# Softmax of a decode attention by chunk instead of by group: a lag of three steps between K and V, and cache reads in runs of 16 KB

## The chip, the cores and the metric

The kernel runs on one core of one Trainium2 chip. The metric is the device time of one execution, in microseconds (us). A time is the median of several runs; a ratio is the mean time of one kernel's fast runs over that of the other's fast runs of the same rounds, so it is not quite the ratio of the medians. The span of a profile is the profiled execution itself; the timed value of that execution is about 1.8 us longer in the two profiles compared.

## The reference, cut to what matters

One token is decoded through a transformer block: modulation, layer norm, attention over a long cache, and a gated feed-forward layer. The cache is nearly all of the data.

```python
B, Sq, D = (1, 1, 1024)
Hq, Hkv, Sk, Dh = (32, 4, 65536, 128)        # 8 query heads share one K/V head
...
sa, ca, ga, sb, cb, gb = ...                  # (silu(c) @ w_mod), six vectors
h = layernorm(x) * (1 + ca) + sa
q = (h @ wq)                                  # heads
scores = einsum('bhqd,bhkd->bhqk', q, k) * Dh ** (-0.5)
p = softmax(scores)
o = einsum('bhqk,bhkd->bhqd', p, v) @ wo
x = x + ga * o
h = layernorm(x) * (1 + cb) + sb
x = x + gb * ((gelu(h @ w_gate) * (h @ w_up)) @ w_down)     # F = 3584
```

K and V together are 134.2 MB in bf16; all inputs read are 185.6 MB.

## The kernel before

The cache of each of the four K/V heads (a "group") is cut into 8 chunks of 8192 keys: 32 K chunks and 32 V chunks of 2 MB. A step handles one K chunk and, `LAG` steps later, the V chunk of the same number. In each of the 16 units of a step, PE transposes four blocks of 128 keys (plus one extra "warm" matmul that is overwritten), DVE or ACT copies the result from PSUM to `kt`, PE multiplies it with the queries, and PE multiplies four V blocks with the probabilities.

```python
E_KEYS = 16                           # keys in a row on one partition: 16 * 128 * 2 B = 4 KB
CH = min(E_KEYS * P * 4, SK)          # 8192
LAG = NCH + 2                         # 10: exp needs the maximum of the whole group of 8 chunks
...
def kv_src(tensor_ap, i):
    g, cch = divmod(i, NCH)
    return tensor_ap[0, g, cch * CH:(cch + 1) * CH, :].rearrange(
        "(a p e) d -> p a (e d)", p=P, e=E_KEYS)
```

One queue issues every load in program order. Each load waits until its buffer is free, and what is behind it waits too:

```python
pro_rot = ["kb0", "kb1", "kb2", "wb0", "wb1", "vb0", "vb1", "vb2"]    # w_mod, wq, the first K chunks
kpool = ["kb0", "kb1", "kb2", "wb0", "wb1"]                           # later K chunks
for st, (ki, vi) in enumerate(steps):
    if ki is not None: ...addjob(("k", ki), ...)
    if vi is not None: addjob(("v", vi), f"vb{vi % 3}")               # V: three buffers
...
def issue(key, dst_fn, src_ap):
    wtv(sy, b.fsem, b.issued)         # the buffer's last user is done
    inst = sy.dma_start(dst_fn(b.t), src_ap)
```

The score copy is on ACT, and the exps of a group come in one burst, 8 of them over 512 columns:

```python
def scatter_copy(i):                  # ACT, once per K chunk
    inst = ac.activation(out=out_ap, in_=in_ap, func=ACT.Copy)
def emit_exp(g, h):                   # ACT, 8 per group
    inst = ac.activation(out=PT[g % 2][:, h, :], in_=S[g % 2][:, h, :], func=ACT.Exp,
                         bias=negm[...], scale=SCALE, accum_out=sums[...])
```

## Time and profile before

| | before |
|---|---|
| time, median of all 16 runs | 484.77 us |
| span of the profile | 482.5 us |
| mean rate of the loads over the span | 387 GB/s |
| steps of K alone | 10 |
| first V chunk used at | 142.1 us |

The first lines are from the page of the kernel before: the span in 40 slices of 12.06 us. A digit is the busy share in tenths, `DMA` is the mean of the 16 engines, `GB/s` is what they moved.

```profile
span 482.5 us, 18072 instructions
...
PE   1345299999779889879898888898898543164342
...
PEclk9999999999989999998799999889999555555555
DMA  8999999999974999999999999999998999999994
GB/s 312 421 423 418 412 408 407 407 408 407 406 289 157 409 408 399 407 408 407 408 407 407 404 400 407 408 408 406 407 376 330 383 410 409 402 418 418 410 387 161
```

The stream of loads is near its top nearly everywhere. The exceptions are slices 12 and 13 (289 and 157 GB/s, at 132.7 to 156.8 us), and weakly slices 30 to 32 (376, 330, 383). The same page has the kinds of work that matter here: line, engine, operation, tiles, shapes, count, busy time, mean ns, then the idle time before it.

```profile
L752 DVE CAST kt<-tb 128x512 bf16<-128x512 f32 x256 | 176.2, 691 | 115.3 <-PE tb L481 113.7
L926 ACT ACTIVATE kt<-tb 128x512 bf16<-128x512 f32 x256 | 150.6, 599 | 128.1 <-PE tb L481 128.0
L351 PE MATMUL pv<-PT,vb 128*128 128x8 bf16 x1536 | 101.5, 176 | 34.5 <-DMA vb<-in_A_v_cache_dram 30.1
...
L936 ACT ACTIVATE S<-sc 128x512 f32<-128x512 f32 x32 | 33.8, 1057 | 10.4 <-PE tb L351 9.6
...
L947 ACT ACTIVATE PT<-S,negm 128x512 bf16<-128x512 f32 x32 | 22.7, 711 | 1.6 <-DVE negm L776 1.6
```

The windows view gives the busy time of each engine in a stretch, with the number of instructions, the granted clock, the DMA share and the rate. These two are the stretch in which the stream starves, for the kernel before:

```profile
132.66:144.72 12.06, 9.56 (x176) 8.75 (x174) 6.39 (x10) 8.78 (x18) 0.00 (x0) 0.86 0.73 290
144.72:156.78 12.06, 12.06 (x298) 11.78 (x295) 8.86 (x16) 7.67 (x14) 0.00 (x0) 1.00 0.44 156
```

In the second one PE (the first busy time) is full for the whole window, while the DMA share is 0.44: here compute is what the stream waits for. The waits view of the load queue of the kernel before says on what (total us, times, longest):

```profile
SPq L299 <- PE pv L536: 184.1, 25, 22.2
```

The queue waited longest for the matmul that ends a V chunk, because the next V load wants that chunk's buffer.

### The profile page before, as it was taken

What the parts mean: (1) busy time and instruction counts of PE and PEld (TensorE: products, weight loads), DVE (VectorE), ACT (ScalarE), POOL (GpSimd) and SP (SyncE); (2) the same over time, 40 slices, a digit from 0 to 9 for tenths busy, and PEclk for the clock granted to TensorE, in tenths of its full rate; (3) what the DMA queues carried; (4) which work ended last, traced back from release to release, by engine and by line L of the source; (5) the groups of instructions that cost most, each with busy time, mean ns of one, the idle gap of its engine ahead of it and who ended that gap; (6) DMA issues with size and microseconds to landing.
All of it is one profiled execution on the core that took longest, in us unless ns stands there. A gap on an engine that the chain in (4) does not pass through costs nothing.

```text
span 482.5 us, 18072 instructions
## 1 busy us (share of the span) xinstructions
PE 345.8 (72%) x8243; PEld 326.6 (68%) x8243; DVE 212.3 (44%) x400; ACT 207.2 (43%) x361; POOL 2.3 (0%) x11
## 2 busy tenths in 40 slices
PE   1345299999779889879898888898898543164342
PEld 1344299998779788879798888798887543163332
DVE  0002068888657656556366565556655100020010
ACT  2000067776976555585355558555555500010000
POOL 0000000000000000000000000000000000000000
PEclk9999999999989999998799999889999555555555
DMA  8999999999974999999999999999998999999994
GB/s 312 421 423 418 412 408 407 407 408 407 406 289 157 409 408 399 407 408 407 408 407 407 404 400 407 408 408 406 407 376 330 383 410 409 402 418 418 410 387 161
DMA packets 46205, 186.77 MB, mean 387 GB/s; under 512 B 1584, under 2 KB 1584, under 8 KB 44080
## 3 DMA queue, kind: packets, MB, share of 16 engines
q1 hardware_dynamic: 46128, 185.61, 96.8%
q8 instruction: 65, 1.06, 0.9%
q14 instruction: 12, 0.10, 0.1%
HBM read 185.60 MB, written 0.00 MB: 385 GB/s over the span
## 4 chain that ended last, share of the span: by engine, by line
PE 54%; DMA 23%; issue 8%; SPq 8%; ACT 6%; DVE 1%; ACTq 0%; DVEq 0%
PE tb L351 30%; DMA vb<-in_A_v_cache_dram 9%; SPq L299 7%; PE sc L351 7%; DMA vb<-in_w_mod_dram 6%; PE pv L351 6%; PE tb L481 6%; DMA kb<-in_B_w_down_dram 4%; DMA kb<-in_A_k_cache_dram 4%; ACT PT L947 3%; ACT kt L926 3%; PE sc L504 2%; PE pv L536 2%; PE pr L351 1%; DVE kt L752 0%
## 5 line engine op out<-in xcount | busy, mean ns | idle before, releaser
L752 DVE CAST kt<-tb 128x512 bf16<-128x512 f32 x256 | 176.2, 691 | 115.3 <-PE tb L481 113.7
L926 ACT ACTIVATE kt<-tb 128x512 bf16<-128x512 f32 x256 | 150.6, 599 | 128.1 <-PE tb L481 128.0
L351 PE MATMUL pv<-PT,vb 128*128 128x8 bf16 x1536 | 101.5, 176 | 34.5 <-DMA vb<-in_A_v_cache_dram 30.1
L351 PE MATMUL sc<-qT,kt 128*128 128x8 bf16 x1536 | 112.4, 167 | 17.6 <-ACT kt L926 12.2
L351 PEld LDWEIGHTS pv<-PT,vb 128*128 128x128 bf16 x1536 | 83.3, 100 | 36.0 <-DMA vb<-in_A_v_cache_dram 31.1
L351 PE MATMUL tb<-ident,kb 128*128 128x128 bf16 x864 | 99.1, 225 | 3.7 <-issue 3.7
L351 PEld LDWEIGHTS sc<-qT,kt 128*128 128x128 bf16 x1536 | 80.9, 97 | 22.0 <-ACT kt L926 13.8
L504 PE MATMUL sc<-qT,kt 128*128 128x8 bf16 x512 | 85.1, 166 | 2.5 <-issue 2.5
L351 PE MATMUL tb<-kb,ident 128*128 128x256 bf16 x288 | 80.0, 278 | 4.1 <-DMA kb<-in_A_k_cache_dram 4.1
L536 PE MATMUL pv<-PT,vb 128*128 128x8 bf16 x512 | 79.7, 175 | 0.0
L351 PEld LDWEIGHTS tb<-ident,kb 128*128 128x128 bf16 x864 | 73.5, 99 | 8.5 <-issue 3.8
L481 PE MATMUL tb<-ident,kb 128*128 128x128 bf16 x288 | 65.0, 226 | 1.8 <-issue 1.8
L351 PE MATMUL tb<-ident,wb 128*128 128x128 bf16 x528 | 59.5, 222 | 1.9 <-issue 1.9
L536 PEld LDWEIGHTS pv<-PT,vb 128*128 128x128 bf16 x512 | 50.2, 98 | 2.1 <-issue 1.9
L504 PEld LDWEIGHTS sc<-qT,kt 128*128 128x128 bf16 x512 | 49.1, 96 | 2.0 <-issue 2.0
L351 PE MATMUL tb<-wb,ident 128*128 128x256 bf16 x176 | 48.2, 274 | 0.0
L351 PEld LDWEIGHTS tb<-ident,wb 128*128 128x128 bf16 x528 | 44.3, 98 | 4.2 <-issue 1.6
L481 PE MATMUL tb<-ident,wb 128*128 128x128 bf16 x176 | 39.3, 223 | 0.9 <-issue 0.9
L936 ACT ACTIVATE S<-sc 128x512 f32<-128x512 f32 x32 | 33.8, 1057 | 10.4 <-PE tb L351 9.6
L351 PEld LDWEIGHTS tb<-kb,ident 128*128 128x128 bf16 x288 | 28.0, 97 | 5.2 <-DMA kb<-in_A_k_cache_dram 4.2
L481 PEld LDWEIGHTS tb<-ident,kb 128*128 128x128 bf16 x288 | 29.1, 101 | 2.3 <-issue 2.3
L947 ACT ACTIVATE PT<-S,negm 128x512 bf16<-128x512 f32 x32 | 22.7, 711 | 1.6 <-DVE negm L776 1.6
(164 smaller groups left out, 258.4 us busy)
## 6 DMA issues: line engine op xcount, KB each, us to landing
vb<-in_A_v_cache_dram SPq DMA_DIRECT2D x32, 2048.0 KB, 14.1
kb<-in_A_k_cache_dram SPq DMA_DIRECT2D x18, 2048.0 KB, 22.5
wb<-in_A_k_cache_dram SPq DMA_DIRECT2D x11, 2048.0 KB, 20.2
wob<-in_A_wo_dram SPq DMA_DIRECT2D x4, 2048.0 KB, 18.4
vb<-in_A_k_cache_dram SPq DMA_DIRECT2D x3, 2048.0 KB, 25.5
kb<-in_B_w_gate_dram SPq DMA_DIRECT2D x3, 1792.0 KB, 21.0
vb<-in_B_w_up_dram SPq DMA_DIRECT2D x3, 1792.0 KB, 29.1
kb<-in_B_w_down_dram SPq DMA_DIRECT2D x3, 1792.0 KB, 20.9
```

Of the source, the lines that this page charges most:

```text
L299: inst = sy.dma_start(dst_fn(b.t), src_ap)
L351: inst = pe.matmul(*args, **kwargs)
L481: last = f(TB[tb][:, bb * P:(bb + 1) * P], tt[:, slot:slot + P], ident[:, :], start=True, stop=True)
L504: last = f(SC[scb][:, b * HPG:(b + 1) * HPG], kt[:, slot0 + bb * P:slot0 + (bb + 1) * P], qT[:, g * HPG:(g + 1) * HPG], start=True, stop=True)
L536: last = f(PVB[0][:, 0:HPG], tt[:, slot:slot + DH], PT[gv % 2][:, :, bq], start=first, stop=final)
L752: inst = dv.tensor_copy(kt[:, slot0:slot0 + BU * P], TB[tb][:, 0:BU * P])
L926: inst = ac.activation(out=kt[:, slot0:slot0 + BU * P], in_=TB[tb][:, 0:BU * P], func=ACT.Copy)
L936: inst = ac.activation(out=out_ap, in_=in_ap, func=ACT.Copy)
L947: inst = ac.activation(out=PT[g % 2][:, h, :], in_=S[g % 2][:, h, :], func=ACT.Exp, bias=negm[:, g * HPG + h:g * HPG + h + 1], scale=SCALE ...
```

## The change

Every chunk gets its own softmax: its own maximum, exps and partial V product, and the eight parts of a group are combined at its end with weights exp(m_c - M). V can then follow K after 3 steps instead of 10. The score copy goes from ACT to DVE. Each partition reads 64 keys in a row (16 KB) instead of four runs of 16 keys (4 KB). Loads of `w_gate` are put between the last V chunks.

```diff
-E_KEYS = 16
+E_KEYS = 64
-    CH = min(E_KEYS * P * 4, SK)
+    CH = min(E_KEYS * P, SK)
-    LAG = NCH + 2
+    LAG = 3
-    NKT = 8
+    NKT = 6
+    NSR = 2
+    NPR = 4
...
             if vi is not None:
+                if ki is None:
+                    addjob(("gate", gates_early), kpool[(kidx + 1 + gates_early) % len(kpool)])
+                    gates_early += 1
                 addjob(("v", vi), f"vb{vi % 3}")
...
-            for g in range(G):
+            for i in range(NKC):
                 inst = gp.partition_all_reduce(gmax..., rmax..., P, bass.bass_isa.ReduceOp.max)
...
-                    last = f(PVB[0][:, 0:HPG], tt[:, slot:slot + DH], PT[gv % 2][:, :, bq],
+                    last = f(GB[gv % 2][:, cv * HPG:(cv + 1) * HPG], tt[:, slot:slot + DH],
+                             PTR[vi % NPR][:, :, b], start=first, stop=final)
...
+            def chunk_sc_copy(i):                                   # DVE
+                inst = dv.tensor_copy(out_ap, in_ap)
...
+            def group_post(gv):                                     # DVE, about ten small operations
+                ... negM = min over chunks, wdel = negm - negM, wexp on ACT,
+                ... ow = sum(part * wexp), tw = sum(total * wexp), oT = ow / tw
...
-                inst = ac.activation(out=PT[g % 2][:, h, :], in_=S[g % 2][:, h, :], func=ACT.Exp,
+                inst = ac.activation(out=PTR[i % NPR][:, h, :], in_=SR[i % NSR][:, h, :], func=ACT.Exp,
```

More of the change, by code (lines that the diff above doesn't have):

```diff
@@ L85, in bass_adaLN_cond__gqa_block_cached__geglu_ffn__decode_kernel @@
     NKC = G * NCH
-    LAG = NCH + 2
+    LAG = 3
     NSTEPS = NKC + LAG
-    NKT = 8
+    NKT = 6
     NTB = 4
     SLAG = 3
+    NSR = 2
+    NPR = 4
     SCALE = float(DH) ** -0.5
     EPS = 1e-5
-    NBQ = SK // P
     WO_ROWS = HPG * DH
@@ L97, in bass_adaLN_cond__gqa_block_cached__geglu_ffn__decode_kernel @@
     assert CH <= STAGE_COLS
+    assert NCH * HPG <= 512
+    SC_COPY_AT = SLAG
+    CMAX_AT = SLAG + 1
+    NEGM_AT = SLAG + 3
+    EXP_AT = SLAG + 5
     with ExitStack() as es:
@@ L104, in bass_adaLN_cond__gqa_block_cached__geglu_ffn__decode_kernel @@
         sem_names = [
-            "misc", "gp", "gpmx", "pe", "dve", "act", "t2act", "t2dve", "ea", "ed", "sdone", "scdone",
+            "misc", "gp", "gpmx", "dve", "act", "t2act", "t2dve", "ea", "ed", "sdone", "scdone",
             "exp", "pr", "pv", "out",
@@ L124, in bass_adaLN_cond__gqa_block_cached__geglu_ffn__decode_kernel @@
         kt = sb("kt", [P, NKT * BU * P])
-        S = [sb(f"S{j}", [P, HPG, NBQ], FP32) for j in range(2)]
-        PT = [sb(f"PT{j}", [P, HPG, NBQ]) for j in range(2)]
+        SR = [sb(f"SR{j}", [P, HPG, NB], FP32) for j in range(NSR)]
+        PTR = [sb(f"PTR{j}", [P, HPG, NB]) for j in range(NPR)]
         x8 = sb("x8", [NI, P])
@@ L142, in bass_adaLN_cond__gqa_block_cached__geglu_ffn__decode_kernel @@
         stat = sb("stat", [P, 8], FP32)
-        rmax = sb("rmax", [P, G * HPG], FP32)
-        cmax = sb("cmax", [P, G * HPG], FP32)
-        gmax = sb("gmax", [P, G * HPG], FP32)
-        negm = sb("negm", [P, G * HPG], FP32)
-        sums = sb("sums", [P, G * HPG], FP32)
+        rmax = sb("rmax", [P, NKC * HPG], FP32)
+        gmax = sb("gmax", [P, NKC * HPG], FP32)
+        negm = sb("negm", [P, NKC * HPG], FP32)
+        sums = sb("sums", [P, NKC * HPG], FP32)
+        negM = sb("negM", [P, HPG], FP32)
+        wdel = sb("wdel", [P, NCH * HPG], FP32)
+        wexp = sb("wexp", [P, NCH * HPG], FP32)
+        cmb1 = sb("cmb1", [P, NCH * HPG], FP32)
+        cmb2 = sb("cmb2", [P, NCH * HPG], FP32)
+        ow = sb("ow", [P, HPG], FP32)
+        tw = sb("tw", [P, HPG], FP32)
         rtot8 = sb("rtot8", [P, HPG], FP32)
@@ L165, in bass_adaLN_cond__gqa_block_cached__geglu_ffn__decode_kernel @@
         SC = [pst(f"sc{j}") for j in range(2)]
-        PVB = [pst("pv")]
-        PR = [pst("pr")]
+        GB = [pst("gb0"), pst("gb1")]
         plan = {}
@@ L229, in bass_adaLN_cond__gqa_block_cached__geglu_ffn__decode_kernel @@
         kidx = None
+        gates_early = 0
         WO_AT_CV = max(0, NCH - 2)
@@ L249, in bass_adaLN_cond__gqa_block_cached__geglu_ffn__decode_kernel @@
                     wo_step[gq] = (s_last + 2) if (s_last + 2) < NSTEPS else None
-        frot = ["kb0", "kb1", "kb2", "wb0", "wb1", "vb0", "vb1", "vb2", "wob"]
-        fidx = 0
+        frot = ["kb2", "wb0", "wb1", "kb0", "kb1", "vb2", "vb0", "vb1", "wob"]
+        assert kpool[(kidx + 1) % len(kpool)] == "kb2"
+        fidx = gates_early
         for kind in ("gate", "up"):
-            for j2 in range(NI // 2):
+            for j2 in range(gates_early if kind == "gate" else 0, NI // 2):
                 addjob((kind, j2), frot[fidx % len(frot)])
@@ L276, in prog_gp @@
             rec("gp_ready", sp.inc(inst, 1))
-            for g in range(G):
-                wt(gp, s["dve"], ("rmax_ready", g))
-                inst = gp.partition_all_reduce(gmax[:, g * HPG:(g + 1) * HPG], rmax[:, g * HPG:(g + 1) * HPG],
+            for i in range(NKC):
+                wt(gp, s["dve"], ("rmax_ready", i))
+                inst = gp.partition_all_reduce(gmax[:, i * HPG:(i + 1) * HPG], rmax[:, i * HPG:(i + 1) * HPG],
                                                P, bass.bass_isa.ReduceOp.max)
-                rec(("gmax_ready", g), s["gpmx"].inc(inst, 1))
+                rec(("gmax_ready", i), s["gpmx"].inc(inst, 1))
         def prog_sync(sy):
@@ L379, in job_end, with pr_use @@
                 definc(b.fsem, ("free", key), inst)
-            pr_banks_list = [PR[0]] + [TB[j] for j in range(NTB)]
-            pr_phase = ["wide"]
+            pr_banks_list = [GB[0][:, :], GB[1][:, :]] + [TB[j][:, :] for j in range(NTB)]
+            pr_rot = [0]
             bank_last_key = {}
-            pr_rot = [0]
             def pr_bank_ap(bank):
                 return pr_banks_list[bank]
-            def pr_use(key):
+            def pr_use(key, fixed_bank=None):
                 k = len(pr_uses)
                 pr_uses.append(key)
-                if pr_phase[0] == "attn":
-                    bank = 0
+                if fixed_bank is not None:
+                    bank = fixed_bank
                 else:
@@ L449, in prog_pe @@
                 job_end(key)
-            pr_phase[0] = "attn"
             bank_last_key.clear()
@@ L464, in emit_T @@
                 tt = kbuf_t[i]
-                g, cch = divmod(i, NCH)
                 tb = U % NTB
@@ L495, in emit_S @@
                     if i >= 2:
-                        wt(pe, s["act"], ("scfree", i - 2))
+                        wt(pe, s["dve"], ("scfree", i - 2))
                 ev = evac_engine(U)
@@ L522, in emit_PV @@
                     vbuf_t[vi] = job_begin(key)
-                    if cv == 0:
-                        wt(pe, s["exp"], ("exp_done", gv))
-                        if gv >= 1:
-                            wt(pe, s["dve"], ("pvfree", gv - 1))
+                    wt(pe, s["exp"], ("exp_done", vi))
+                    if cv == 0 and gv >= 2:
+                        wt(pe, s["dve"], ("prfree", ("woacc", gv - 2)))
                 tt = vbuf_t[vi]
@@ L530, in emit_PV @@
                     b = u * BU + bb
-                    bq = cv * NB + b
                     slot = blk_slot(b)
-                    first = (cv == 0 and b == 0)
-                    final = (cv == NCH - 1 and b == NB - 1)
+                    first = (b == 0)
+                    final = (b == NB - 1)
                     f = pe.matmul if bb == BU - 1 else mm
-                    last = f(PVB[0][:, 0:HPG], tt[:, slot:slot + DH], PT[gv % 2][:, :, bq],
-                             start=first, stop=final)
+                    last = f(GB[gv % 2][:, cv * HPG:(cv + 1) * HPG], tt[:, slot:slot + DH],
+                             PTR[vi % NPR][:, :, b], start=first, stop=final)
                 if u == NU - 1:
-                    if cv == NCH - 1:
-                        rec(("pv_done", gv), s["pv"].inc(last, 1))
-                        job_end(key)
-                    else:
-                        job_end(key, last)
-            def group_tot(gv):
-                wt(pe, s["exp"], ("exp_done", gv))
-                bank, k = pr_use(("tot", gv))
-                inst = pe.matmul(pr_bank_ap(bank)[:, 0:HPG], ones_f[:, :], sums[:, gv * HPG:(gv + 1) * HPG],
-                                 start=True, stop=True)
+                    rec(("pv_done", vi), s["pv"].inc(last, 1))
+                    job_end(key)
+            def group_tot(gv):
+                i_last = gv * NCH + NCH - 1
+                wt(pe, s["exp"], ("exp_done", i_last))
+                bank, k = pr_use(("tot", gv), fixed_bank=gv % 2)
+                inst = pe.matmul(GB[gv % 2][:, NCH * HPG:2 * NCH * HPG], ones_f[:, :],
+                                 sums[:, gv * NCH * HPG:(gv + 1) * NCH * HPG], start=True, stop=True)
                 pr_done(("tot", gv), inst)
@@ L555, in group_wo @@
                 tt = job_begin(key)
-                bank, k = pr_use(("woacc", gv))
+                bank, k = pr_use(("woacc", gv), fixed_bank=gv % 2)
                 prb = pr_bank_ap(bank)
@@ L599, in prog_pe @@
                 group_wo(gv0)
-            pr_phase[0] = "wide"
-            last_attn_key = bank_last_key.get(0)
+            last_keys = dict(bank_last_key)
             bank_last_key.clear()
-            if last_attn_key is not None:
-                for bbk in range(len(pr_banks_list)):
-                    bank_last_key[bbk] = last_attn_key
-            pr_rot[0] = 1
+            for bbk in range(len(pr_banks_list)):
+                bank_last_key[bbk] = ("woacc", G - 1)
+            pr_rot[0] = 2
             wt(pe, s["dve"], "ln2_part1_ready")
@@ L641, in chain_wait @@
                 wtv(dv, sd, sd.count)
-            pr_banks_list_d = [PR[0]] + [TB[j] for j in range(NTB)]
+            pr_banks_list_d = [GB[0][:, :], GB[1][:, :]] + [TB[j][:, :] for j in range(NTB)]
             def prbank(key):
@@ L647, in prbank @@
                     return pr_banks_list_d[pr_use_bank[key]]
-                return PR[0]
+                return GB[0][:, :]
             def pr_wait(key):
@@ L753, in emit_evac @@
                 rec(("evac_done", U), s["ed"].inc(inst, 1))
+            def chunk_sc_copy(i):
+                wt(dv, s["scdone"], ("scdone", i))
+                if i >= NSR:
+                    wt(dv, s["exp"], ("exp_done", i - NSR))
+                out_ap = SR[i % NSR][:, :, :].rearrange("p h b -> p b h")
+                in_ap = SC[i % 2][:, 0:NB * HPG].rearrange("p (b h) -> p b h", h=HPG)
+                inst = dv.tensor_copy(out_ap, in_ap)
+                v = done(inst)
+                rec(("sccopied", i), v)
+                rec(("scfree", i), v)
@@ L755, in chunk_max @@
             def chunk_max(i):
-                g, cch = divmod(i, NCH)
-                wt(dv, s["act"], ("sccopied", i))
                 chain_wait()
-                if cch == 0:
-                    target = rmax[:, g * HPG:(g + 1) * HPG]
-                else:
-                    target = cmax[:, g * HPG:(g + 1) * HPG]
-                inst = dv.tensor_reduce(out=target, in_=S[g % 2][:, :, cch * NB:(cch + 1) * NB], axis=AX.X,
-                                        op=ALU.max)
-                done(inst)
@@ L766, in chunk_max @@
-                if cch > 0:
-                    chain_wait()
-                    inst = dv.tensor_tensor(out=rmax[:, g * HPG:(g + 1) * HPG], in0=rmax[:, g * HPG:(g + 1) * HPG],
-                                            in1=target, op=ALU.max)
-                    done(inst)
-                if cch == NCH - 1:
-                    rec(("rmax_ready", g), sd.count)
-            def group_negm(g):
-                wt(dv, s["gpmx"], ("gmax_ready", g))
-                inst = dv.tensor_scalar(out=negm[:, g * HPG:(g + 1) * HPG], in0=gmax[:, g * HPG:(g + 1) * HPG],
-                                        scalar1=-SCALE, scalar2=None, op0=ALU.mult)
-                rec(("negm_ready", g), done(inst))
@@ L780, in group_post, with chunk_negm @@
-            def group_post(gv):
+                inst = dv.tensor_reduce(out=rmax[:, i * HPG:(i + 1) * HPG], in_=SR[i % NSR][:, :, :], axis=AX.X,
+                                        op=ALU.max)
+                rec(("rmax_ready", i), done(inst))
+            def chunk_negm(i):
+                wt(dv, s["gpmx"], ("gmax_ready", i))
+                inst = dv.tensor_scalar(out=negm[:, i * HPG:(i + 1) * HPG], in0=gmax[:, i * HPG:(i + 1) * HPG],
+                                        scalar1=-SCALE, scalar2=None, op0=ALU.mult)
+                rec(("negm_ready", i), done(inst))
@@ new lines, in group_post @@
+            def group_post(gv):
+                ncol = NCH * HPG
+                base = gv * ncol
+                gb = GB[gv % 2]
+                i_last = gv * NCH + NCH - 1
+                wtv(dv, sd, plan.get(("negm_ready", i_last), 0))
+                inst = dv.tensor_reduce(out=negM[:, :], in_=negm[:, base:base + ncol].rearrange("p (c h) -> p h c", h=HPG),
+                                        axis=AX.X, op=ALU.min)
+                done(inst)
+                chain_wait()
+                negM_b = bass.AP(tensor=negM, offset=0, ap=[[negM.ap().ap[0][0], P], [0, NCH], [1, HPG]])
+                inst = dv.tensor_tensor(out=wdel[:, :].rearrange("p (c h) -> p c h", h=HPG),
+                                        in0=negm[:, base:base + ncol].rearrange("p (c h) -> p c h", h=HPG),
+                                        in1=negM_b, op=ALU.subtract)
+                rec(("wdel_ready", gv), done(inst))
+                wt(dv, s["act"], ("wexp_ready", gv))
+                wt(dv, s["pv"], ("pv_done", i_last))
@@ L781, in group_post @@
                 pr_wait(("tot", gv))
-                inst = dv.reciprocal(rtot8[:, :], prbank(("tot", gv))[:, 0:HPG])
-                done(inst, True)
-                wt(dv, s["pv"], ("pv_done", gv))
+                inst = dv.tensor_tensor(out=cmb1[:, :], in0=gb[:, 0:ncol], in1=wexp[:, :], op=ALU.mult)
+                done(inst)
                 chain_wait()
-                inst = dv.tensor_tensor(out=oT[:, gv * HPG:(gv + 1) * HPG], in0=PVB[0][:, 0:HPG],
-                                        in1=rtot8[:, :], op=ALU.mult)
@@ L788, in group_post @@
-                v = done(inst)
-                rec(("oT_ready", gv), v)
-                rec(("pvfree", gv), v)
+                inst = dv.tensor_reduce(out=ow[:, :], in_=cmb1[:, :].rearrange("p (c h) -> p h c", h=HPG),
+                                        axis=AX.X, op=ALU.add)
+                done(inst)
+                inst = dv.tensor_tensor(out=cmb2[:, :], in0=gb[:, ncol:2 * ncol], in1=wexp[:, :], op=ALU.mult)
+                v = done(inst, True)
+                rec(("pvfree", gv), v)
@@ new lines, in group_post @@
+                chain_wait()
+                inst = dv.tensor_reduce(out=tw[:, :], in_=cmb2[:, :].rearrange("p (c h) -> p h c", h=HPG),
+                                        axis=AX.X, op=ALU.add)
+                done(inst)
+                chain_wait()
+                inst = dv.reciprocal(rtot8[:, :], tw[:, :])
+                done(inst)
+                chain_wait()
+                inst = dv.tensor_tensor(out=oT[:, gv * HPG:(gv + 1) * HPG], in0=ow[:, :], in1=rtot8[:, :], op=ALU.mult)
@@ L792, in group_attn @@
+                rec(("oT_ready", gv), done(inst))
             def group_attn(gv):
@@ L800, in group_attn @@
                 done(inst, True)
+            pending_sc = []
             pending_cm = []
@@ L814, in prog_dve @@
                             emit_evac(U)
+                    while pending_sc and pending_sc[0][0] <= (st, u):
+                        _, ic = pending_sc.pop(0)
+                        chunk_sc_copy(ic)
                     while pending_cm and pending_cm[0][0] <= (st, u):
@@ L817, in prog_dve @@
                         chunk_max(ic)
-                        gg, cc = divmod(ic, NCH)
-                        if cc == NCH - 1:
-                            pending_negm.append(((st, u + 2), gg))
                     while pending_negm and pending_negm[0][0] <= (st, u):
-                        _, gg = pending_negm.pop(0)
-                        group_negm(gg)
+                        _, ic = pending_negm.pop(0)
+                        chunk_negm(ic)
                     while pending_attn and pending_attn[0][0] is not None and pending_attn[0][0] <= (st, u):
@@ L827, in prog_dve @@
                 if ki is not None:
-                    pending_cm.append(((st + 1, NU // 2), ki))
+                    pending_sc.append(((st + 1, SC_COPY_AT), ki))
+                    pending_cm.append(((st + 1, CMAX_AT), ki))
+                    pending_negm.append(((st + 1, NEGM_AT), ki))
                 if vi is not None:
@@ L834, in prog_dve @@
                         pending_attn.append(((ws, 1) if ws is not None else None, gv))
+            for _, ic in pending_sc:
+                chunk_sc_copy(ic)
             for _, ic in pending_cm:
                 chunk_max(ic)
-                gg, cc = divmod(ic, NCH)
-                if cc == NCH - 1:
-                    pending_negm.append((None, gg))
-            for _, gg in pending_negm:
-                group_negm(gg)
+            for _, ic in pending_negm:
+                chunk_negm(ic)
             for _, gg in pending_post:
@@ L927, in emit_evac @@
                 rec(("evac_done", U), s["ea"].inc(inst, 1))
-            def scatter_copy(i):
-                g, cch = divmod(i, NCH)
-                wt(ac, s["scdone"], ("scdone", i))
-                if g >= 2 and cch == 0:
-                    wt(ac, s["exp"], ("exp_done", g - 2))
-                out_ap = S[g % 2][:, :, cch * NB:(cch + 1) * NB].rearrange("p h b -> p b h")
-                in_ap = SC[i % 2][:, 0:NB * HPG].rearrange("p (b h) -> p b h", h=HPG)
-                inst = ac.activation(out=out_ap, in_=in_ap, func=ACT.Copy)
-                v = sa.inc(inst, 1)
-                rec(("sccopied", i), v)
-                rec(("scfree", i), v)
@@ L941, in emit_exp @@
-            def emit_exp(g, h):
-                if h == 0:
-                    wt(ac, s["dve"], ("negm_ready", g))
-                    wt(ac, sa, ("sccopied", g * NCH + NCH - 1))
-                    if g >= 2:
-                        wt(ac, s["pv"], ("pv_done", g - 2))
-                inst = ac.activation(out=PT[g % 2][:, h, :], in_=S[g % 2][:, h, :], func=ACT.Exp,
-                                     bias=negm[:, g * HPG + h:g * HPG + h + 1], scale=SCALE,
-                                     accum_out=sums[:, g * HPG + h:g * HPG + h + 1])
+            def emit_exp(i, h):
+                if h == 0:
+                    wt(ac, s["dve"], ("negm_ready", i))
+                    wt(ac, s["dve"], ("sccopied", i))
+                    if i >= NPR:
+                        wt(ac, s["pv"], ("pv_done", i - NPR))
+                inst = ac.activation(out=PTR[i % NPR][:, h, :], in_=SR[i % NSR][:, h, :], func=ACT.Exp,
+                                     bias=negm[:, i * HPG + h:i * HPG + h + 1], scale=SCALE,
+                                     accum_out=sums[:, i * HPG + h:i * HPG + h + 1])
@@ L950, in emit_exp, with group_wexp @@
                 v2 = s["exp"].inc(inst, 1)
                 if h == HPG - 1:
-                    rec(("exp_done", g), v2)
-            pending_sc = []
+                    rec(("exp_done", i), v2)
+            def group_wexp(gv):
+                wt(ac, s["dve"], ("wdel_ready", gv))
+                inst = ac.activation(out=wexp[:, :], in_=wdel[:, :], func=ACT.Exp, scale=-1.0)
+                rec(("wexp_ready", gv), sa.inc(inst, 1))
             pending_exp = []
+            pending_wexp = []
@@ L956, in prog_act @@
             for st, (ki, vi) in enumerate(steps):
+                while pending_wexp and pending_wexp[0][0] <= st:
+                    _, gg = pending_wexp.pop(0)
+                    group_wexp(gg)
                 for u in range(NU):
@@ L961, in prog_act @@
                             emit_evac(U)
-                    while pending_sc and pending_sc[0][0] <= (st, u):
-                        _, ic = pending_sc.pop(0)
-                        scatter_copy(ic)
-                        gg, cc = divmod(ic, NCH)
-                        if cc == NCH - 1:
-                            for h in range(HPG):
-                                uu = NU // 2 + 3 + h
-                                pending_exp.append(((st + uu // NU, uu % NU), gg, h))
                     while pending_exp and pending_exp[0][0] <= (st, u):
-                        _, gg, hh = pending_exp.pop(0)
-                        emit_exp(gg, hh)
+                        _, ic, hh = pending_exp.pop(0)
+                        emit_exp(ic, hh)
                 if ki is not None:
-                    pending_sc.append(((st + 1, 2), ki))
-            for _, ic in pending_sc:
-                scatter_copy(ic)
-                gg, cc = divmod(ic, NCH)
-                if cc == NCH - 1:
-                    for h in range(HPG):
-                        pending_exp.append((None, gg, h))
-            for _, gg, hh in pending_exp:
-                emit_exp(gg, hh)
+                    for h in range(HPG):
+                        uu = EXP_AT + h
+                        pending_exp.append(((st + 1 + uu // NU, uu % NU), ki, h))
+                if vi is not None:
+                    gv, cv = divmod(vi, NCH)
+                    if cv == NCH - 1:
+                        pending_wexp.append((st + 1, gv))
+            for _, ic, hh in pending_exp:
+                emit_exp(ic, hh)
+            for _, gg in pending_wexp:
+                group_wexp(gg)
             wt(ac, s["dve"], "ln2_var_ready")
```

## The prediction

> **What bounds the kernel now.** The DMA stream. The slices show the DMA engines over 90% busy almost throughout; steady attention (157 to 350 us) moves 407 GB/s, while PE is busy about 10.4 of each 12.06 us. Where PE is full (144.7 to 156.8 us, 298 matmuls), a whole step (one K and one V chunk, 208 matmuls) takes about 8.4 us of PE; its 4.19 MB take 10.3 us at 407 GB/s. So attention is DMA-bound with PE slack. The stream starves twice: 132.7 to 156.8 us (290 and 156 GB/s: about 11 us lost), and weakly at 350 to 386 us (375, 330, 384 GB/s: about 4 us). The first exists because ten K chunks (7.36 us each) run before any V chunk is consumed: V fills its three buffers and the in-order queue stops (it waits on the PV line for 184 us in total).
>
> **What the change does.**
> 1. Lag from K to V falls from 10 steps to 3, so from about 80 us K and V are consumed in pairs: the first starvation vanishes, -11 us. Three gate loads go between the last V chunks, into free K buffers: most of the second, -3 us.
> 2. Each partition reads 16 KB in one run instead of four of 4 KB. In this trace the rate follows the run length: 2 KB (w_down) 387 GB/s, 4 KB (K, V) 407, about 8 KB (wq, gate) 411 to 418, 12 KB (w_mod) 422. A line through 4 and 12 KB per engine gives 8.6 ns per packet plus 26.9 GB/s, and hits the 2 KB rate; for 16 KB it gives 424 GB/s (estimate). 134.2 MB of cache take 316 us instead of 330: -13 us. [...]
> 3. Exp is split: 256 of 64 columns instead of 32 of 512. Tanh over 28 columns took 0.23 us, accumulator read 0.19: at most 3.6 us per step. ACT loses the score copy (1.06). Per step: 8 evictions (0.60) + exps, at most 8.4 us, under 9.9.
> 4. DVE gets the score copy (estimate 0.7 to 1.1 us) and a negm per chunk (0.17), loses a max merge: about 7.4 us per step. POOL's reduction (0.37 us) fits between max and negm.
> 5. Group combines add about ten small DVE operations (0.2 us each): hidden by buffers.
>
> **Critical path.** 1 and 2 lie on it, 3 to 5 do not, while a step's compute stays under 9.9 us. Sum: start 3, w_mod 30, wq 20, K and V 316, wo 21.5, gate and up 35.5, w_down 19, landings 4, after the last load 5: 454 us of span; the timed value was 1.5 us over the span.
>
> **Predicted: 456 us, 448 to 466 in 8 of 10.** Faster by over 2%: 0.94; within 2%: 0.05; slower: 0.01.
>
> **What shows it right.** Slices after 60 us at about 424 GB/s with no dip at 132 to 157; span end 5 us after the last w_down landing; ACT 6.5 to 8.4 and DVE 7 to 7.5 us per step; PE waiting for V chunks in each step.
>
> **What would make it wrong.** 16 KB runs no faster than 4 KB (+10 us). ACT or DVE holding evictions so that a step exceeds 9.9 us (each 0.5 us costs 16 us). A lower granted clock (0.76 was seen at 229 to 241 us) for most of attention[...].

What a granted clock of 0.76 does to a step was not shown by the trace that the prediction was made from; no_warm, below, with less work on PE, ran at a mean of 0.76 and took 460.44 us. The estimate for the score copy on DVE lies between two times of the page before, 691 ns for an eviction on DVE and 1057 ns for that copy on ACT.

## The result, and the profile after

| | before | after |
|---|---|---|
| time, median | 484.77 us (16 runs) | 460.95 us (9 runs) |
| ratio after/before | | 0.9513 (0.9496 to 0.9530) |
| span | 482.5 us | 458.8 us |
| mean rate over the span | 387 GB/s | 407 GB/s |
| packets of K and V | 32768 of 4 KB, median 161 ns | 8192 of 16 KB, median 613 ns |
| first V chunk used at | 142.1 us | 84.8 us |
| last V chunk landed at | 422.9 us | 413.4 us |

It is faster by 4.9%, inside the predicted range but 5 us over the predicted 456. These are the lines of the page after that answer to those shown before; a slice is now 11.47 us:

```profile
span 458.8 us, 18628 instructions
...
PE   1335379998888987999888997888888989705554
...
PEclk9999999999999997898999989999999899855555
DMA  7999999999999999999999999999999999999993
GB/s 307 420 425 421 429 423 424 422 426 430 425 414 413 424 421 427 423 421 421 406 427 426 422 423 426 406 395 412 426 428 426 416 393 392 400 421 418 404 386 118
```

The hole at 132 to 157 us is gone. Outside of a few dips, the slices of attention now read 420 to 430 GB/s instead of 407. The groups of the page after:

```profile
L760 DVE CAST kt<-tb 128x512 bf16<-128x512 f32 x256 | 175.6, 688 | 111.1 <-PE tb L495 110.6
L960 ACT ACTIVATE kt<-tb 128x512 bf16<-128x512 f32 x256 | 151.1, 591 | 124.6 <-PE tb L495 123.2
L368 PE MATMUL gb<-PTR,vb 128*128 128x8 bf16 x1536 | 114.5, 176 | 21.3 <-DMA vb<-in_A_v_cache_dram 13.1
...
L969 ACT ACTIVATE PTR<-SR,negm 128x64 bf16<-128x64 f32 x256 | 86.2, 340 | 6.6 <-DVE negm L782 6.5
...
L969 ACT ACTIVATION_READ_ACCUMULATOR PTR<-SR,negm 128x1 f32 x256 | 49.1, 192 | 0.0
...
L769 DVE COPY SR<-sc 128x512 f32<-128x512 f32 x32 | 33.3, 1040 | 2.3 <-PE tb L368 1.3
```

An exp over 64 columns took 340 ns and its accumulator read 192; the score copy took 1040 ns on DVE where it had taken 1057 on ACT. The waits view of the kernel after holds a surprise:

```profile
PEld tb L368 <- issue: 21.2, 16, 2.9
PEld gb L368 <- issue: 15.4, 14, 1.9
PEld gb L368 <- DMA vb<-in_A_v_cache_dram: 13.3, 2, 12.8
```

These are waits of PE's weight loads (PEld), and "issue" is a stop for which the profile shows no cause. PE waited for V chunks only twice, and 12.8 us of that is for the very last chunk; it stopped for "issue" far more often. The prediction had expected a wait for V in each step. The next table, worked out from the landing times of the loads and the first matmul on each chunk, says how long each V chunk lay in its buffer before use:

```
V chunk            0    1    2    3    7    8   10   14   15   20   28   29   30   31
before   us     24.3 22.7 21.1 12.1  5.1  6.4  8.9  7.2  1.1  3.8  0.0  0.0  0.0  0.0
after    us      5.2  4.7  3.1  4.1  0.5  0.8  7.0  7.2  1.6  6.7  6.8  6.7  0.0  0.0
```

V chunks arrive only a few us before they are used, but they do arrive first, so the picture alone does not tell whether the stream or PE sets the time after the change. The experiments have to.

### The profile page after: what moved, and what is told of

It reads as the page before. It is cut to its first block, busy times and chain, and to the rows that moved or that the text cites. A ratio compares the mean times of both kernels' runs of the same rounds, so it can differ in the third digit from the quotient of the medians.

```text
span 458.8 us, 18628 instructions
## 1 busy us (share of the span) xinstructions
PE 342.8 (75%) x8243; PEld 325.6 (71%) x8243; DVE 239.6 (52%) x456; ACT 236.7 (52%) x781; POOL 12.6 (3%) x39
## 3 DMA queue, kind: packets, MB, share of 16 engines
q8 instruction: 65, 1.06, 0.9%
## 4 chain that ended last, share of the span: by engine, by line
PE 62%; DMA 18%; issue 10%; DVE 4%; SPq 3%; ACT 2%; DVEq 0%
PE tb L368 34%; PE gb L368 9%; PE sc L368 8%; DMA vb<-in_w_mod_dram 6%; PE tb L495 6%; DMA vb<-in_A_v_cache_dram 4%; DMA wb<-in_B_w_down_dram 4%; DMA kb<-in_A_k_cache_dram 4%; SPq L316 3%; PE gb L548 3%; PE sc L518 3%; ACT PTR L969 1%; DVE kt L760 1%; ACT kt L960 0%; DVE rmax L776 0%
## 5 line engine op out<-in xcount | busy, mean ns | idle before, releaser
L368 PE MATMUL gb<-PTR,vb 128*128 128x8 bf16 x1536 | 114.5, 176 | 21.3 <-DMA vb<-in_A_v_cache_dram 13.1
L368 PE MATMUL tb<-ident,kb 128*128 128x128 bf16 x960 | 109.3, 223 | 5.2 <-issue 5.2
L368 PEld LDWEIGHTS gb<-PTR,vb 128*128 128x128 bf16 x1536 | 91.6, 99 | 24.3 <-DMA vb<-in_A_v_cache_dram 13.3
L368 PE MATMUL tb<-kb,ident 128*128 128x256 bf16 x320 | 88.3, 276 | 5.0 <-DMA kb<-in_A_k_cache_dram 3.9
L368 PEld LDWEIGHTS tb<-ident,kb 128*128 128x128 bf16 x960 | 81.2, 98 | 12.3 <-issue 7.3
L969 ACT ACTIVATE PTR<-SR,negm 128x64 bf16<-128x64 f32 x256 | 86.2, 340 | 6.6 <-DVE negm L782 6.5
L548 PE MATMUL gb<-PTR,vb 128*128 128x8 bf16 x512 | 86.6, 175 | 2.9 <-issue 2.9
L368 PEld LDWEIGHTS sc<-qT,kt 128*128 128x128 bf16 x1536 | 77.4, 96 | 12.8 <-issue 5.9
L495 PE MATMUL tb<-ident,kb 128*128 128x128 bf16 x320 | 71.9, 225 | 2.0 <-issue 2.0
L368 PE MATMUL tb<-ident,wb 128*128 128x128 bf16 x576 | 65.1, 222 | 2.9 <-issue 2.9
L368 PE MATMUL tb<-wb,ident 128*128 128x256 bf16 x192 | 52.5, 274 | 1.5 <-issue 1.2
L548 PEld LDWEIGHTS gb<-PTR,vb 128*128 128x128 bf16 x512 | 49.4, 97 | 2.8 <-issue 2.8
L969 ACT ACTIVATION_READ_ACCUMULATOR PTR<-SR,negm 128x1 f32 x256 | 49.1, 192 | 0.0
L495 PE MATMUL tb<-ident,wb 128*128 128x128 bf16 x192 | 42.8, 223 | 1.3 <-issue 1.3
L769 DVE COPY SR<-sc 128x512 f32<-128x512 f32 x32 | 33.3, 1040 | 2.3 <-PE tb L368 1.3
## 6 DMA issues: line engine op xcount, KB each, us to landing
wob<-in_A_wo_dram SPq DMA_DIRECT2D x4, 2048.0 KB, 18.9
```

The lines of the kernel that those rows point to most:

```text
L368: inst = pe.matmul(*args, **kwargs)
L495: last = f(TB[tb][:, bb * P:(bb + 1) * P], tt[:, slot:slot + P], ident[:, :], start=True, stop=True)
L548: last = f(GB[gv % 2][:, cv * HPG:(cv + 1) * HPG], tt[:, slot:slot + DH], PTR[vi % NPR][:, :, b], start=first, stop=final)
L769: inst = dv.tensor_copy(out_ap, in_ap)
L969: inst = ac.activation(out=PTR[i % NPR][:, h, :], in_=SR[i % NSR][:, h, :], func=ACT.Exp, bias=negm[:, i * HPG + h:i * HPG + h + 1], scale ...
```

## The experiments

Each kernel gave a correct result. A ratio is always to the kernel before, run on the same chip. Differences in us below are between medians; where they are small and the runs come from two calls, the ratios are the safer guide (0.01 is about 4.8 us).

| label | what it is | median us | ratio to before |
|---|---|---|---|
| (the change) | | 460.95 | 0.9513 |
| short_runs | the change with 4 KB runs | 473.80 | 0.9762 |
| long_runs_only | before with 16 KB runs | 481.90 | 0.9925 |
| lag10 | the change with lag 10 | 472.66 | 0.9745 |
| lag10_short | lag 10, 4 KB runs, no early gates | 481.78 | 0.9922 |
| lag10_no_gates | lag 10, no early gates | 478.22 | 0.9880 |
| no_early_gates | the change without early gates | 465.52 | 0.9598 |
| no_warm | the change without the extra matmul | 460.44 | 0.9492 |
| pe_more_after | the change with a longer extra matmul | 461.73 | 0.9543 |
| pe_more_before | before with a longer extra matmul | 490.85 | 1.0142 |
| dve_double | the change, score copy done twice | 460.81 | 0.9497 |
| down_long | the change, w_down in 14 KB runs | 460.96 | 0.9498 |
| tuned | three edits in the tail | 458.62 | 0.9466 |

### Run length alone, in both orders

The first takes the changed kernel back to short runs, the second gives long runs to the kernel before:

```diff
 short_runs (on the change)             long_runs_only (on the kernel before)
-E_KEYS = 64                            -E_KEYS = 16
+E_KEYS = 16                            +E_KEYS = 64
-CH = min(E_KEYS * P, SK)               -CH = min(E_KEYS * P * 4, SK)
+CH = min(E_KEYS * P * 4, SK)           +CH = min(E_KEYS * P, SK)
```

> The changed kernel with the 4 KB runs of the kernel before (order, lag and chunked softmax as changed). Theory (the DMA stream sets the time): K and V packets go back from 8192 of 613 ns to 32768 of 161 ns, over 16 engines 314 to 330 us, so +16 us: 477 us, no dip in the slices, about 407 GB/s. Rival (compute sets the step now, because PE hardly ever waits for a V chunk in the changed trace): run length matters little, under 466 us.

> The kernel before with 16 KB runs only. Theory: up to 157 us the stream is held by compute (ten K chunks first), so faster packets gain nothing there and only deepen the dip; the gain is that of some 22 later steps, about 9 to 11 us: 474 us. Rival (the two parts add up independently): -16 us, 469 us.

The short runs cost the changed kernel 12.9 us (473.80 against 460.95), so the rival "compute sets the step" falls. The expected 16 us was too much: taken from rates, 134.2 MB at 407.5 and at 424 GB/s differ by 12.8 us (estimate), which is what was measured.

In the old order the same runs gained only 3.3 us (481.90 against 485.21), which fits neither expectation. This is the page of long_runs_only, to be held against the slices of the kernel before:

```profile
GB/s 314 422 424 418 427 431 422 425 416 425 425 180 151 427 425 379 434 423 423 427 386 379 414 424 423 426 426 414 418 244 348 378 415 418 413 417 416 409 386 138
```

The stream is indeed faster wherever it runs freely (423 to 427 GB/s), but both holes got deeper: 180 and 151 GB/s at 132 to 157 us, and 244, 348 and 378 at 349 to 385 us. The consumer kept its pace: V chunk 21, whose K-and-V step is the last full one, was first used at 363.0 us, and at 361.5 us in the kernel before. The faster stream only ran further ahead (V chunk 20 lay 11.3 us in its buffer instead of 3.8), then found its buffers full. So run length and order are not two independent gains: alone they give 3.3 us, and 11.4 us for everything but run length (485.21 to 473.80); together 24. The gain of the runs is as small at lag 10 in the changed code: 3.6 us by the medians of lag10_short and lag10_no_gates (481.78 to 478.22), 2 us by their ratios (0.9922 and 0.9880), which is within the noise of the two.

### The lag, and what is left without it

```diff
 lag10
-    LAG = 3
+    LAG = 10
-    NPR = 4
+    NPR = 11
-                if ki is None:
+                if ki is None and gates_early < 3:
 lag10_short: the same, with gates_early < 0 (none), E_KEYS = 16 and CH = E_KEYS * P * 4
 lag10_no_gates: as lag10, with gates_early < 0 (none)
 (buffers of the later loads are taken in the order in which they fall free)
```

> The changed kernel with a lag of 10 steps (and 11 probability buffers instead of 4), early gates held to 3. Theory (the lag made the dip): the dip near 132 to 157 us returns with at least the 11 us of the kernel before, 471 to 474 us. Rival (chunked softmax, not the lag, removed the dip): within 2 us of 461.

> The changed kernel with lag 10, 4 KB runs and no early gates: what is left is the chunked softmax with its moved score copy. Theory (that is off the path): within 3 us of the kernel before, 482 to 488 us. Rival (spreading the exps and combining later is itself worth time): under 479 us.

> The changed kernel with lag 10 and no early gates, runs of 16 KB. Theory (at lag 10 the hole among the last V chunks is larger, and the early gates fill it): 480 us, 7 to 8 us over the lag 10 run with gates. Rival (early gates are worth the same 4.6 us at any lag): 477 us.

With lag 10 the time is 472.66 us, 11.7 us more than the change, as expected from the lag and not from chunked softmax. The slices of lag10 show the hole back in its place:

```profile
GB/s 309 424 423 420 426 426 426 425 421 332 419 365 116 426 427 388 431 424 422 427 368 388 419 413 422 426 426 422 424 388 399 423 424 401 408 410 417 410 386 156
```

What chunked softmax did apart from lag, run length and gates was worth 3.4 us (lag10_short, 481.78 against 485.21; by the interval of the ratio, 0.9887 to 0.9958, some 2 to 5.5 us), between theory and rival and a little outside the theory's range. The traces show where one part comes from. In the kernel before the eight exps of the first group stand in one burst on ACT between evictions, and the step that holds the burst took 14.0 us; in lag10_short the step in that place took 8.8 us. Against that, its K-only steps took 7.8 us instead of 7.4, so the first V chunk was used only about 2.5 us sooner in lag10_short (139.6 against 142.1 us). No run isolates the burst.

At lag 10 the early gates are worth 5.6 us by the medians (478.22 to 472.66) and 6.5 us by the ratios (0.9880 and 0.9745), with some 2 us of noise. That lies between the expectations, 7 to 8 and 4.6, and does not decide between them.

### The early gates

```diff
 no_early_gates
-                if ki is None:
+                if ki is None and gates_early < 0:
                     addjob(("gate", gates_early), ...)
```

> The changed kernel with no gate loads between the last V chunks. Theory: the stream runs short while the last V chunks wait for their three buffers, +2 to +4 us, seen as slices under 400 GB/s before the last V chunk lands: 463 to 465 us. Rival (with a lag of 3 only three V-only steps are left, so nothing is gained by the early gates): within 1 us of 461.

It took 465.52 us, 4.6 us more than the change, a little over what was expected. The hole stands where it should, in two slices (313 and 276 GB/s), just before the last V chunk:

```profile
DMA  7999999999999999999999999999999977999994
GB/s 310 421 423 422 424 428 427 420 422 427 427 412 420 423 420 425 427 426 422 404 425 425 426 425 422 407 387 425 423 424 422 424 313 276 417 419 418 408 386 156
```

### Is PE on the path?

The extra matmul of each unit is an easy handle on PE: it changes the work of PE alone (and, as it turned out, the granted clock: a mean of 0.91 in the change, 0.76 without it, 0.93 with the longer one).

```diff
 no_warm                 pe_more_after, pe_more_before
-    WARM_N = 256        -    WARM_N = 256
+    WARM_N = 0          +    WARM_N = 384
```

> The changed kernel without the extra 256-column matmul per unit (its result is overwritten). Theory (DMA sets the time): within 1.5 us of 461, with V chunks landing no earlier and PE waiting for them more. Rival (PE sets the step): 512 matmuls of about 0.11 us less, about 1.7 us per step, so the time falls by more than 5 us until the stream's own limit.

> The changed kernel with 384 instead of 256 columns in the extra matmul of each unit, about 0.85 us more of PE per step. Theory of the prediction (a step of PE is 8.4 us, so there is room below the stream's 9.9): within 1.5 us of 461. Rival (the steady step of PE is about 10.2 us because PE also stops about 1 us at every 128th matmul and runs at a lower granted clock at times, so hardly any room is left): up to 29 x 0.6 us more, 470 to 480 us.

> The same on the kernel before. Theory of the prediction (ten K-only steps bound by compute, then bound by the stream with PE slack): +8 to 10 us, 494 us. Rival (compute also set the pace of the 22 full steps up to 362 us, which is why longer runs alone gained only 3 us): +0.85 us on all 32 steps, 508 to 514 us.

The 0.11 us per extra matmul and the 0.85 us per step are estimates. They agree with the page of the kernel before: a matmul of 256 columns took 278 ns there and one of 128 columns 225 ns, so 53 ns for 128 columns, 0.85 us for 16 of them. The lower clock that the rival names was a mean of 0.96 between 157 and 350 us in the change.

Without it the time is 460.44 us, and now the stream is plainly the limit: most V chunks were used less than 2.5 us after they landed, many at once. The last V chunk landed at 412.0 us, 1.3 us sooner than in the change. The granted clock fell, from a mean of 0.91 to 0.76 over the span, and the time did not care:

```profile
PEclk9999999976797576787865859596787785655555
DMA  7999999999999999999999999999999999999992
GB/s 310 418 424 420 430 423 424 426 425 426 421 417 413 428 423 425 421 423 425 408 427 422 426 425 427 421 411 407 422 429 423 426 414 418 391 423 418 379 362 102
```

How near PE is to the path shows in the chain of work that ended last, which the page follows back from the end. These are its shares of the span by engine, first of the change, then of no_warm:

```profile
PE 62%; DMA 18%; issue 10%; DVE 4%; SPq 3%; ACT 2%; DVEq 0%
```

```profile
PE 38%; DMA 33%; SPq 13%; DVE 6%; issue 6%; ACT 3%; DVEq 0%; ACTq 0%
```

In the change the chain runs mostly through PE and its stops, and one could take PE for the limit. With less work on PE it moves over to the loads, and the time falls by 0.5 us (1 us by the ratios): PE and the stream are near balance, and relieving PE alone gains next to nothing.

With a longer extra matmul the changed kernel took 461.73 us, within the range that the prediction's theory gave; the rival's 470 to 480 us falls. So after the change there is room on PE, and the longer matmul was absorbed. The trace shows by what: PE worked more and stopped less. These are the lines of its waits view that answer to the first two shown for the change (21.2 and 15.4 us):

```profile
PEld tb L368 <- issue: 14.6, 27, 3.1
PEld gb L368 <- issue: 10.2, 11, 1.9
```

Between 160 and 345 us, the stops of PE's weight loads over 0.25 us sum to 27.8 us in the change (22.8 of it "issue") and to 18.0 us with the longer matmul (14.5).

The kernel before took 6.6 us more (490.85 against 484.25). Its theory had +8 to +10 us, mostly the ten K-only steps. The ordinary ones grew from 7.4 to 7.9 us, the nine before the burst of exps by 5.6 us together, while the step with the burst shrank by 0.9 us; the first V chunk was used 4.9 us later (147.0 against 142.1 us). The rival's 24 us or more falls: the full steps absorbed the extra work here too (stops of 25.8 us, 18.9 of them "issue", fell to 13.2 and 7.8 us in the same stretch).

The "issue" stops come in one pattern. Most lie 126 to 128 weight loads apart (or a multiple of that, where one is shorter than 0.25 us), whatever the kernel does between them. A weight load and its matmul are two instructions, so that is some 256 instructions. The instruction queue moved 65 packets, each of 16384 bytes, in the change, and 61 in no_warm, which has 512 matmuls and 512 weight loads fewer: four packets for 1024 instructions, or one for 256 (estimate from these counts). The lines of the two pages (packets, MB, share of the 16 engines' span):

```profile
q8 instruction: 65, 1.06, 0.9%
```

```profile
q8 instruction: 61, 1.00, 0.9%
```

The times of these packets tie the stops to them: of the 23 "issue" stops of the change between 160 and 345 us, 22 ended 1.1 to 1.7 us after such a packet had ended. While the stream is full, such a stop took 0.86 us on average in the kernel before and 0.99 us in the change, and there were 6.3 to 6.4 us from packet to packet in the change, the kernel before, and both kernels with more PE work. In the window at 144.7 to 156.8 us of the kernel before, where the stream stood at 156 GB/s, there were no stops, and two steps took 8.6 us each instead of about 10.5. The two packets next to and in that window took no less time themselves (1.33 and 1.22 us, against a median of 1.08), so the difference does not lie in the transfer of the packet. Why PE stops at these points, and less while the stream is idle, was not shown; no run took these packets away alone.

### Is DVE on the path?

```diff
 dve_double
+                done(dv.tensor_copy(SX[:, :, :].rearrange("p h b -> p b h"), in_ap))
                 inst = dv.tensor_copy(out_ap, in_ap)
```

> The changed kernel with the score copy done twice on DVE (once into a scratch tile): +1.04 us of DVE per step, 33 us in all. Theory (DVE is off the path): within 1.5 us of 461. Rival (evictions on DVE gate the PE step, which is the pace): about +1 us per step, up to 490 us.

SX is a scratch tile that nothing reads. It took 460.81 us: 26 us more of busy DVE (265.9 against 239.6 us) cost nothing. The step has room on DVE.

### A better tail

Since the stream sets the end, its slowest packets are the next target: `w_down` in runs of 2 KB at 386 GB/s.

```diff
 down_long
-    tt[:, ci * F + t * P:ci * F + (t + 1) * P]
+    tt[:, c0:c0 + 7 * (P - 1) + 1:7]          # c0 = ci*F + (t//7)*7*P + t%7
-    B_w_down[k0 * P:k1 * P, :].rearrange("(ci p) n -> p ci n", p=P)
+    B_w_down[k0 * P:k1 * P, :].rearrange("(p ci) n -> p ci n", ci=7)
 (shortened: 7 stands for NDD and for the number of rows of 128 in the load)
```

> The changed kernel with w_down read in runs of 14 KB instead of 2 KB (hidden features reordered so that a partition owns seven consecutive rows; the gate and up weights are read with a stride of 7 columns). Theory (the stream sets the tail, 8.6 ns per packet and 26.9 GB/s per engine): w_down falls from 18.7 to about 17 us, so -2 us: 459 us. Rival (strided weight loads on PE cost more than that): no gain or a loss.

No gain, 460.96 us. The loads did get shorter: the four of `w_down` landed 4.3 us apart instead of about 4.65. But reading gate and up weights with a stride of seven columns slowed PE. The groups by form of the change and then of down_long, for one load of `w_up` or `w_gate` and 55 of its 56 weight loads (the figures after the bar: time in which at least one of them ran, in us, and the mean ns of one):

```profile
L368 PEld LDWEIGHTS tb<-h2T,wb 128*128 128x128 bf16 x55 | 1.5, 104 | 0.0
```

```profile
L368 PEld LDWEIGHTS tb<-h2T,wb 128*128 128x128 bf16 x55 | 3.0, 153 | 0.0
```

One weight load took 153 ns instead of 104, and since they overlap, 55 of them filled 3.0 us instead of 1.5, at a granted clock of 0.5 in both. Why the stride slows them was not shown; tuned, below, mostly with a stride of eight, had 157 to 159 ns. PE became the end of the kernel: with gates starting at 424.6 us because the last V chunk lands so late, its 8 loads at 3.0 us end at 448.7 us, and the matmuls of `w_down` then run back to back to 456.7 us, 3.4 us after the last load landed (453.3 us).

The last kernel removes that: the last three V chunks go into free K buffers ahead of all gates, so that PE can start the gates sooner; `w_down` is read in runs of 16 KB, with a last load of half the size.

```diff
 tuned
-    NDD = 7
+    NDD = 8
                 if ki is None:
-                    addjob(("gate", gates_early), kpool[(kidx + 1 + gates_early) % len(kpool)])
-                    gates_early += 1
-                addjob(("v", vi), f"vb{vi % 3}")
+                    v_late += 1
+                    addjob(("v", vi), kpool[(kidx + v_late) % len(kpool)])
+                else:
+                    addjob(("v", vi), f"vb{vi % 3}")
 (cut: v_late starts at 0, buffers of the later loads in a new order;
  w_down as in down_long, with 8, 8, 8 and 4 rows of 128 per load)
```

> The changed kernel with three edits in the tail: the last three V chunks go into free K buffers, ahead of all gate loads; w_down is read in runs of 16 KB, with the hidden features reordered; its last load is 4 rows of 128 instead of 7. Theory (the tail with long w_down runs was bound by strided weight loads on PE, which start late because the last V chunk comes late; with V first they start some 9 us sooner): the stream sets the end again, w_down 1.5 us shorter, last load 0.7 us less of PE: 458.5 us. Rival (strided loads still bound the tail): 460 us or more.

The expected 0.7 us less of PE agree with the page of the change, where 55 matmuls of a `w_down` load took 1.6 to 1.8 us: 24 fewer take 0.7 us (estimate). The kernel took 458.62 us (458.28 to 458.84), below the fastest run of the change (460.39); the ratios to the kernel before are 0.9466 (0.9452 to 0.9480) and 0.9513 (0.9496 to 0.9530). The last V chunk landed at 400.2 us instead of 413.4, the gates began at 414.3 us, and from there the stream set the pace again. The three edits were not run apart, so the 2.3 us cannot be shared out among them. Its slices hold to the end:

```profile
span 456.5 us, 18628 instructions
...
DMA  8999999999999999999999999999999999999992
GB/s 309 421 421 422 431 424 426 423 426 425 421 417 413 424 426 422 424 422 415 403 423 424 429 419 406 410 404 413 425 423 426 424 421 411 385 420 419 422 426 122
```

## Why the prediction was right

The direction, the size and the mechanism held: 460.95 us against 456, in a range of 448 to 466.

- *The stream bounds the kernel, and its hole comes from ten K chunks ahead of any V.* Shown: the hole came back with lag 10 and went with lag 3 (11.7 us; predicted 11).
- *16 KB runs give 424 GB/s, -13 us.* Shown at lag 3: 12.9 us, and the median packet took 613 ns where the line of the prediction gives 618. But the prediction gave this as a gain of its own. It is worth 3.3 us in the old order, so the two items of its list depend on each other; the total was right because both were done at once.
- *Early gates, -3 us.* Shown, 4.6 us (4.1 by the ratios).
- *ACT and DVE stay under a step.* Shown: between 157 and 350 us they were busy 128.3 and 128.0 us of 193, about 7.1 us of each step of 10.7 us, as costed. Doubling the score copy on DVE changed nothing.
- *PE needs 8.4 us per step and waits for V in each.* The sign named did not appear. That figure was read from a window in which the stream stood half idle. With a full stream PE also stops about once per 128 matmuls (0.86 us on average in the kernel before, 0.99 us in the change), and full steps took about 10.5 us in the kernel before, more than the 9.9 us that the prediction allowed. The conclusion (PE off the path) still held, because the stops shrank when PE had more to do (27.8 to 18.0 us between 160 and 345 us). The prediction did not foresee that, so this part of it was luck.
- *Softmax by chunk is neutral.* Not quite: 3.4 us of gain, measured at lag 10, that was in no term of the sum.

The missing 5 us sit mostly in attention, as the landing times show:

| landed | predicted sum | measured |
|---|---|---|
| last w_mod | 33 | 34.8 |
| last wq | 53 | 54.7 |
| last V (316 for K and V, 21.5 wo, 13 for three gates) | 404 | 413.4 |
| last w_down (with the 4 us put in for landings) | 449 | 454.0 |
| end of the span | 454 | 458.8 |

The stretch from the last wq to the last V took 358.7 us instead of 351. The 4 us set aside for landings covered half of that. Of what is in it and was in no term, the instruction packets can be named: 1.06 MB in the whole kernel, about 2.5 us at 424 GB/s, or 4 us by the time that their packets took, 0.9% of the 16 engines' span (both estimates). The rest shows as dips: from 57 to 401 us the slices fall short of 424 GB/s by 4.9 us, of which about 2 us were foreseen, for the 2 KB rows of wo (86 ns a packet, 381 GB/s over 16 engines). Why the other dips (406 and 395 GB/s at 287 to 310 us, 393 and 392 at 367 to 390 us) are so deep was not settled.

Also open: what holds full steps at about 10.5 us in long_runs_only, where the stream could do better. The stops of PE about once per 128 matmuls are the candidate; no run tested it.

## What to carry to other kernels

When a kernel lives on one stream of loads, ask first which consumer's order lets its buffers fill up: here a stage that consumed one of two inputs alone stalled the stream (289 and 157 GB/s), and faster loads only made the hole deeper (180 and 151 GB/s). Longer runs per partition paid off once the order was right (12.9 us, against 3.3 us in the old order); the cost of a packet could be fitted from other loads of the same trace (median packets of 2, 4, 8 and 12 KB took 86, 161, 312 and 460 ns before, and those of 16 KB then took 613 ns). Read an engine's time per step from a stretch in which the other limits are as they will be, not from one in which the memory stood half idle, and test "off the path" by adding work to the engine.
